# Attention, gated convolution and two-way mixing on one core: new engines and a new order for the channel MLP's preparing work

## The chip, the cores and the metric

The kernel runs on one core of a Trainium2 chip. Five engines work at once, each through its own list of instructions in order: TensorE (PE, matmul; its weight loads are listed as PEld), VectorE (DVE), ScalarE (ACT), GpSimd (POOL) and SyncE (SP, which here only issues transfers). They wait for one another by semaphores. The metric is the device time of one launch in microseconds (us); the median of three runs of the kernel before is 745.95 us. Under 0.2% (1.5 us) two kernels here cannot be told apart.

## The reference

```python
def _attn_ref(q, k, v, s):                    # 4 batches, 8 heads, 576 tokens, 64 wide
    cum = np.cumsum(np.maximum(s, 0.0), axis=-1)
    bias = -(cum[:, :, :, None] - cum[:, :, None, :])
    scores = np.matmul(q, k.transpose(0, 1, 3, 2)) / np.sqrt(D)
    scores = np.where(causal, -1e9, scores + np.minimum(bias, 0.0))
    attn = softmax(scores)
    return np.matmul(attn, v)

def _moe_ref(x, w_val, conv_w, w_out):        # x: 4 x 576 tokens x 512 channels
    gate = sigmoid(causal_conv5(x, conv_w))
    return (gate * (x @ w_val)) @ w_out

def _moe2_ref(x, U, V, w_ch1, w_ch2):         # U 576x32, V 32x576, w_ch1 512x2048
    u = x + (x.transpose(0, 2, 1) @ U @ V).transpose(0, 2, 1)
    return u + np.maximum(u @ w_ch1, 0.0) @ w_ch2
```

Attention's output goes through `_moe_ref`, and that through `_moe2_ref`; everything is float32.

## The kernel before, in words

**Number format.** Each float32 operand of a large product is split into a high and a low part of the type that PE multiplies fast (fp32r). `rnd` (L187) rounds to the high part, `rest` (L198) takes the low part, and a product is three matmuls: high by high, high by low, low by high (`three`). So each operand costs a rounding and a subtraction on some engine before PE can start on it.

**Stages.** Until about 295 us the 32 heads of attention run (scores `sc`, exponentials `P`, transposes `pt`, `av`), and beside them the dense work of batches that are done: convolution and gate, `w_val` and `w_out`, and the token mixing with U and V (`nh`/`nl` are the split transposes, `ast` the split product with U, then 16 matmuls `d<-V4h,ast` and `d<-V4l,ast`, added to the residual `uT` on line L766). For the last batch the dense work ends near 365 us. Then comes the channel MLP, to the end at 743 us.

**The channel MLP.** The hidden width of 2048 is cut into 16 blocks, two to a group, 8 groups (g). The 2304 tokens are cut into five tiles: 0 to 3 of 512 and tile 4 of 256. For each tile and block, `ch1` makes 12 matmuls into a PSUM tile `d`; ACT takes the relu and rounds (`hh`), DVE takes the rest (`hl`); `ch2` makes 12 matmuls into the four accumulators `acc0` to `acc3`, two blocks behind each other in the same accumulators, and after the second block DVE adds each to `uT` (L1076). `acc0` and `acc1` have two PSUM buffers of their own, `acc2` and `acc3` share the six of `d`. `ch2` runs two blocks behind `ch1` (`LAG`). From group 1 on, tiles 2 and 3 are done together by seven products in place of eight (`seven`). Those need sums of the two tiles' tokens (`token_sums`, L935: names `sn`, and `Th`/`Tl` for their parts; two sets, made once) and sums of quarters of each weight group (`weight_sums`, L957: `Sh`/`Sl`, made for each group).

**The transition.** The blocks of tiles 0 to 2 of group 0 (`EARLY` = 3) are mixed into the last batch's dense work, so that PE has something to do while that work waits for other engines; how many goes by the rates `R2` and `R3`. What is left of group 0, and after it the groups 1 to 7, runs in the closing loop. In that loop `token_sums` is emitted, two steps for each step of the MLP, and `split_u` makes the split parts `u` of tile 2, 3 and 4 when the tile comes up.

**Weights.** A weight arrives as 64-bit numbers and is turned into two fp32r parts by `widen` (L421), nine steps for each of 32 pieces: `wd_a` scales the high words (`scr<-raw`), `wd_lim` limits them, four `wd` steps (L429, L430, L433, L434) shift and mask, then `wd_hi` rounds (`w1h` or `w2h`), `wd_rest` takes what is left (`scr<-scr,w1h`) and `wd_lo` adds the low word (`w1l`, `w2l`). 28 of these pieces are made in the MLP, beside PE's work.

**What sets the order.** Each operation has a kind. The table `PLAN` gives every kind an engine and a priority offset, `FIRST` another one during the first heads; the class `Via` (L171) looks it up as the operation is emitted. A scheduler then lays all instructions out by a timeline and these priorities, and each engine executes its list in that order, waiting at the first instruction that is not ready. Helper lines: L185 issues with a priority, L192 and L196 are `rnd` on ACT and on POOL, L201 is `rest`.

Of the kernel before, what the change touches and what calls it, by code (L numbers as in the profile page):

```python
# [21 lines left out]

PLAN = {'pace': ['gpsimd', 6000],
 'qk_hi': ['gpsimd', 100],
 'qk_lo': ['gpsimd', 100],
 'put': ['sync', 3000],
 'wd_rest': ['gpsimd', 0],
 'xh': ['gpsimd', 2000],
 'xl': ['gpsimd', -2000],
 'gh': ['scalar', -2000],  # L30
 'gl': ['vector', 0],
 'uh': ['gpsimd', 0],
 'ul': ['gpsimd', -6000],
 'u4': ['vector', 0],
 'wd_a': ['gpsimd', 0],
 'wd_lim': ['gpsimd', -2000],
 'wd': ['vector', 0],
# [16 lines left out]
 'rb': ['scalar', -100],
 'x': ['vector', -500],
 'tap0': ['scalar', -6000],
 'tap': ['vector', 100],
# [5 lines left out]
 'nh': ['scalar', 0],
 'nl': ['vector', 100],
 'ah': ['scalar', 2000],
 'al': ['vector', 500],
# [69 lines left out]
DT = {'exp': 1.05,
 'xh': 0.32,
 'xl': 0.73,
 'tap': 1.81,
 'taps': 0.44,  # L140
 'tanh': 2.68,
 'gv': 4.87,
 'nl': 1.45,
 'rows': 8.01,
 'prep': 3.36}
# [1066 lines left out]
```

## Time and profile before

| | |
|---|---|
| Runs, us | 745.33, 745.95, 745.99; median 745.95 |
| Profiled execution, us | 745.39, of which the span of the instructions is 743.6 |
| Mean granted clock of PE | 0.993 of full speed |
| Busy share of the span | PE 97%, PEld 82%, DVE 70%, ACT 39%, POOL 53% |

The profile comes from the one execution of 745.39 us. Its span runs from the first to the last instruction; 1.8 us lie around it. A granted clock of 1.00 is 2.4 GHz, one of 0.50 is 1.2 GHz. Busy time of POOL is rough. `out<-in` names what an instruction writes and reads.

### The profile page before, as it was taken

Reading aid. Unit: us, or ns where it says so; the run is one execution under the profiler, and the core shown is the slowest. Engines: PE = TensorE matmul, PEld = TensorE weight load, DVE = VectorE, ACT = ScalarE, POOL = GpSimd, SP = SyncE. Lnnn points to the kernel's source line nnn. Section 1 sums busy time; section 2 is a strip of 40 time slices with the busy share of each in tenths; the row PEclk is TensorE's granted clock in tenths of the full one; section 3 lists DMA queues with packets and bytes.
Section 4 is the critical chain, followed back from the end, with each engine's and each line's share of the span. In section 5 each row is a group of like instructions: output and inputs, shape, how many; then the busy total and the mean of one; then the engine's idle time right before and its main releaser. Section 6 shows DMA issues by size and latency. Waiting matters only on the chain.

```text
span 743.6 us, 12205 instructions
## 1 busy us (share of the span) xinstructions
PE 721.1 (97%) x4327; PEld 609.3 (82%) x4327; DVE 519.4 (70%) x1148; ACT 292.1 (39%) x761; POOL 393.0 (53%) x435
## 2 busy tenths in 40 slices
PE   8898999999999999999979999999999999999998
PEld 5666888789988998898758888888888888888887
DVE  6897988898678656751798696876847657475354
ACT  6677566766687677422221212111212112111120
POOL 2778677666544243640386768757728357181000
PEclk9999999999999999999989999999999999999999
DMA  4665455654556341100001121211101101100023
GB/s 115 200 191 150 121 142 125 161 131 123 138 144 163 91 100 35 58 30 1 1 0 61 53 61 54 85 41 54 49 28 58 57 28 51 37 1 0 15 99 142
DMA packets 27000, 59.38 MB, mean 80 GB/s; under 512 B 4648, under 2 KB 5288, under 8 KB 26940
## 3 DMA queue, kind: packets, MB, share of 16 engines
q1 hardware_dynamic: 26940, 58.61, 27.8%
q8 instruction: 34, 0.56, 0.3%
q14 instruction: 26, 0.21, 0.1%
HBM read 37.04 MB, written 5.31 MB: 57 GB/s over the span
## 4 chain that ended last, share of the span: by engine, by line
PE 82%; DVE 10%; issue 2%; DMA 2%; ACT 2%; POOL 1%; SPq 0%; POOLq 0%; DVEq 0%
PE d L185 38%; PE acc L185 26%; PE pt L185 7%; PE sc L185 5%; PE av L185 5%; DVE av L185 2%; DVE P L185 2%; DVE sn L185 1%; DMA qk<-in_kT 1%; DVE uT L434 1%; DVE Tl L185 1%; ACT P L185 1%; DVE uT L430 0%; DVE uT L1076 0%; DMA uT<-in_w 0%
## 5 line engine op out<-in xcount | busy, mean ns | idle before, releaser
L1076 DVE TENSOR_TENSOR uT<-acc,uT 128x512 f32<-128x512 f32 (+1 forms) x160 | 96.1, 630 | 56.8 <-PE acc L185 56.7
L185 PE MATMUL d<-u,w1h 128*128 128x512 f32 (+1 forms) x464 | 130.2, 366 | 1.1 <-POOL u L185 1.1
L185 PE MATMUL acc<-hl,w2h 128*128 128x512 f32 (+1 forms) x320 | 117.2, 370 | 0.0
L185 PE MATMUL acc<-hh,w2l 128*128 128x512 f32 (+1 forms) x320 | 114.7, 370 | 0.0
L185 PE MATMUL acc<-hh,w2h 128*128 128x512 f32 (+1 forms) x320 | 110.9, 375 | 3.0 <-DVE uT L1076 3.0
L981 ACT ACTIVATE hh<-d 128x512 fp32r<-128x512 f32 (+1 forms) x59 | 31.6, 539 | 186.9 <-PE d L185 147.3
L185 ACT ACTIVATE P<-P,nm 128x576 f32<-128x576 f32 (+4 forms) x160 | 89.1, 559 | 32.7 <-DVE nm L185 32.0
L185 PEld LDWEIGHTS d<-u,w1h 128*128 128x128 f32 x464 | 83.7, 191 | 16.6 <-POOL u L185 2.2
L185 PE MATMUL sc<-K,Q 68*128 68x288 f32 (+13 forms) x384 | 86.6, 338 | 0.3 <-ACT PTA L192 0.2
L185 PE MATMUL d<-u,w1l 128*128 128x512 f32 (+1 forms) x232 | 84.4, 365 | 0.0
L185 PE MATMUL pt<-ident,P 128*128 128x128 f32 x480 | 75.0, 279 | 5.5 <-ACT P L185 3.0
L185 DVE CUSTOM_DVE_ANT_0 P<-sc,causal 64x64 f32<-64x64 f32 (+4 forms) x160 | 64.3, 420 | 22.2 <-PE sc L185 19.1
L185 DVE SCALAR_TENSOR_TENSOR hl<-d,hh 128x512 fp32r<-128x512 f32 (+1 forms) x59 | 36.0, 613 | 58.5 <-ACT hh L981 58.4
L185 PEld LDWEIGHTS acc<-hh,w2h 128*128 128x128 f32 x320 | 60.3, 189 | 14.9 <-issue 3.3
L185 PEld LDWEIGHTS acc<-hh,w2l 128*128 128x128 f32 x320 | 59.8, 188 | 11.6
L185 PEld LDWEIGHTS acc<-hl,w2h 128*128 128x128 f32 x320 | 60.1, 188 | 11.2
L185 PEld LDWEIGHTS sc<-K,Q 68*128 68x128 f32 (+2 forms) x384 | 61.6, 191 | 8.6 <-issue 1.3
L185 PEld LDWEIGHTS pt<-ident,P 128*128 128x128 f32 x480 | 55.2, 142 | 12.2 <-ACT P L185 5.0
L185 DVE SCALAR_TENSOR_TENSOR av<-X,cw,av 128x576 f32<-128x576 f32 x64 | 52.2, 815 | 2.5 <-ACT av L185 2.1
L185 PEld LDWEIGHTS d<-u,w1l 128*128 128x128 f32 x232 | 44.2, 191 | 7.4
L185 POOL TENSOR_SCALAR w2h<-scr 128x512 fp32r<-128x512 f32 x14 | 10.1, 723 | 72.9 <-PE acc L185 53.1
L185 POOL TENSOR_TENSOR Q<-qk,hi 128x576 fp32r<-128x576 f32 x22 | 31.7, 1439 | 16.8 <-PE sc L185 16.8
(170 smaller groups left out, 1587.1 us busy)
## 6 DMA issues: line engine op xcount, KB each, us to landing
raw<-in_w SPq DMA_DIRECT2D x28, 512.0 KB
K<-hi SPq DMA_DIRECT2D x44, 144.0 KB
...
```

The source lines that it names most:

```text
L185: return f(*args, **kw)
L434: lambda: Via("wd").scalar_tensor_tensor(t, raw[..., 0], 2.0 ** -52, t, op0=ALU.mult, op1=ALU.mult),
L981: Via("hh").activation(h_, o, AF.Relu)
L1076: Via("acc").tensor_add(u, o, u)
```

## The change

A third table, `LAST`, holds for what is emitted after the last head, that is for `split_u` and the whole MLP. By it the rounding of the token parts (`uh`), the first step of widening (`wd_a`) and the rounding of weights (`wd_hi`) go from POOL to ACT, and the step behind the rounding (`wd_rest`) from POOL to DVE. In `PLAN` the low part of the weight sums (`sl`) goes from DVE to POOL. Token sums are emitted one step for each MLP step instead of two (`PACE`). Group 0 takes tile 4 before tile 3, and groups 2 to 7 take the tiles in the order 0, 1, 2, 3, 4 instead of 0, 2, 3, 1, 4; group 1 had that order already. Most priorities are new, as are the numbers `R2`, `R3`, `SIDE` and `DT`, by which work is mixed. The kind `tm` of the token mixing's matmuls is split into `tu` (U) and `tv` (V). The arithmetic is the same, and PE and SP have as many instructions as before. ACT gets 72 more and DVE 18 more, POOL 90 fewer. Up to the end of attention PE's order is the same but for a few neighbours that change places. Cut to what the text speaks of:

```diff
-PLAN = {'pace': ['gpsimd', 6000],
+PLAN = {'pace': ['gpsimd', 2000],
...
- 'uh': ['gpsimd', 0],
+ 'uh': ['gpsimd', 6000],
 'ul': ['gpsimd', -6000],
...
- 'wd_lim': ['gpsimd', -2000],
+ 'wd_lim': ['gpsimd', 2000],
 'wd': ['vector', 0],
 'wd_hi': ['gpsimd', -2000],
...
- 'hl': ['vector', -100],
+ 'hl': ['vector', -6000],
 'acc': ['vector', 0],
- 'tc': ['vector', -100],
- 'th': ['scalar', 0],
- 'tl': ['vector', 500],
+ 'tc': ['vector', 500],
+ 'th': ['scalar', -500],
+ 'tl': ['vector', 2000],
...
- 'sl': ['vector', 100],
- 'sn': ['scalar', 2000],
+ 'sl': ['gpsimd', 100],
+ 'sn': ['scalar', 0],
...
-R2 = 0.38
-R3 = 9.68
+R2 = 0.27
+R3 = 10.65
...
-PLACE = [[0, 1, 2, 3, 4], [0, 2, 3, 1, 4]]
+PACE = 1
+PLACE = [[0, 1, 2, 4, 3], [0, 1, 2, 3, 4], [0, 1, 2, 3, 4]]
...
+LAST = {'uh': ['scalar', 500],
+ 'wd_a': ['scalar', -6000],
+ 'wd_hi': ['scalar', 0],
+ 'ox': ['scalar', -2000],
+ 'pt20': ['vector', 500],
+ 'rb': ['vector', 2000],
+ 'c2': ['tensor', -6000],
+ 'acc': ['vector', -100],
+ 'sh': ['scalar', -6000],
+ 'c1': ['tensor', -2000],
+ 'sc': ['gpsimd', -500],
+ 'nh': ['scalar', 100],
+ 'wd_rest': ['vector', 0],
+ 'wd': ['vector', 6000],
+ 'pt30': ['vector', 2000]}
...
-            self.name, self.ahead = FIRST.get(kind, PLAN[kind]) if PLAN[kind][0] != "sync" and phase[0] <= 8 else PLAN[kind]
+            self.name, self.ahead = FIRST.get(kind, PLAN[kind]) if PLAN[kind][0] != "sync" and phase[0] <= 8 else LAST.get(kind, PLAN[kind]) if phase[0] == NH else PLAN[kind]
...
-        for t in range(NB) if g == 0 else PLACE[g > 1]:
+        for t in PLACE[min(g, 2)]:
...
-            for _ in range(2):
+            for _ in range(PACE):
...
-        assert i < 2 * D_ + 1 or not sums2
+        assert i < 2 * PLACE[0].index(D_) + 2 or not sums2
```

The lists below are the engines' orders as built; lines of the changed kernel lie 26 further down.

**PE, ahead of the last batch's V stage** (`d<-V4h,ast`). `acc_4905` and `acc_4921` belong to tile 1, `acc_5045` and `acc_5051` to tile 2. Before:

```order
L185 MATMUL d<-nh,U_68 128x512
L185 MATMUL d<-nl,U_68 128x512
L185 MATMUL acc_5045<-hh,w2h 128x512
L185 MATMUL acc_5045<-hl,w2h 128x512
L185 MATMUL acc_5045<-hh,w2l 128x512
L185 MATMUL d<-nh,U_68 128x512
L185 MATMUL acc_5051<-hh,w2h 128x512
L185 MATMUL acc_5051<-hl,w2h 128x512
L185 MATMUL acc_5051<-hh,w2l 128x512
L185 MATMUL d<-nl,U_68 128x512
L185 MATMUL d<-V4h,ast 128x288
```

After (`acc_4932`, `acc_4936` belong to tile 1):

```order
L211 MATMUL acc_4932<-hh,w2h 128x512
L211 MATMUL acc_4936<-hh,w2h 128x512
L211 MATMUL d<-nh,U_68 128x512
L211 MATMUL acc_4932<-hl,w2h 128x512
L211 MATMUL acc_4936<-hl,w2h 128x512
L211 MATMUL acc_4932<-hh,w2l 128x512
L211 MATMUL acc_4936<-hh,w2l 128x512
L211 MATMUL d<-nl,U_68 128x512
L211 MATMUL d<-V4h,ast 128x288
```

Tile 2's six `acc` matmuls, and 12 of its `ch1` matmuls a little further up, are no longer ahead of the V stage but behind it.

**ACT, from the last batch's `ast` on.** `u` are the high parts of tiles 3 and 4, `Sh` here a buffer that holds a high part of tile 3. Before:

```order
L185 ACTIVATE ast<-d 128x512
L192 ACTIVATE Th_4989<-sn_5005 128x512
L192 ACTIVATE Th_4993<-sn_5007 128x512
L192 ACTIVATE Th_4991<-sn_5006 128x512
L981 ACTIVATE hh<-d 128x512
L192 ACTIVATE Th_4994<-sn_5069 128x512
L192 ACTIVATE Th_4990<-sn_5067 128x512
L192 ACTIVATE Th_4995<-sn_5006 128x512
L981 ACTIVATE hh<-d 128x512
```

After:

```order
L211 ACTIVATE ast<-d 128x512
L211 ACTIVATE u_4419<-uT 128x256
L211 ACTIVATE u_4421<-uT 128x256
L1007 ACTIVATE hh<-d 128x512
L211 ACTIVATE Sh_4985<-uT 128x512
L211 ACTIVATE u_5009<-uT 128x256
L211 ACTIVATE Sh_4985<-uT 128x512
L211 ACTIVATE u_5128<-uT 128x512
L218 ACTIVATE w1h<-scr_5070 128x512
L211 ACTIVATE Th_4989<-sn_5005 128x512
L211 ACTIVATE u_5011<-uT 128x256
L211 ACTIVATE u_5130<-uT 128x512
```

The roundings of `u` and of `w1h` stood in POOL's list before and stand in ACT's now, among the `Th`.

**DVE, up to the first add of an accumulator of tile 2** (`acc_5045` before, `acc_5042` after). Before:

```order
L185 TENSOR_TENSOR sn_5067<-uT,u_4868 128x512
L185 TENSOR_TENSOR Tl_4999<-sn_5006,Th_4991 128x512
L185 SCALAR_TENSOR_TENSOR hl<-d,hh 128x512
L185 TENSOR_TENSOR sn_5069<-uT 128x512
L185 TENSOR_TENSOR sn_5067<-sn_5067,u_4869 128x512
L185 TENSOR_TENSOR sn_5006<-u_4870,sn_5006 128x512
L185 TENSOR_TENSOR Tl_5002<-sn_5069,Th_4994 128x512
L185 TENSOR_TENSOR sn_5006<-sn_5006,u_4871 128x512
L185 TENSOR_TENSOR Tl_4998<-sn_5067,Th_4990 128x512
L1076 TENSOR_TENSOR uT<-acc_5045,uT 128x512
L185 TENSOR_TENSOR Tl_5003<-sn_5006,Th_4995 128x512
```

After:

```order
L211 TENSOR_TENSOR sn_5006<-sn_5006,u_4887 128x512
L211 TENSOR_TENSOR Tl_5002<-sn_5126,Th_4994 128x512
L211 SCALAR_TENSOR_TENSOR hl<-d,hh 128x256
L211 SCALAR_TENSOR_TENSOR scr_5108<-scr_5108,scr_5109 128x512
L211 TENSOR_TENSOR Tl_4998<-sn_5124,Th_4990 128x512
L211 SCALAR_TENSOR_TENSOR hl<-d,hh 128x256
L211 TENSOR_TENSOR Tl_5003<-sn_5006,Th_4995 128x512
L211 TENSOR_SCALAR scr_5109<-scr_5108 128x512
L211 TENSOR_TENSOR sn_5125<-uT,sn_5124 128x512
L211 SCALAR_TENSOR_TENSOR scr_5109<-raw,scr_5109 128x512
L227 TENSOR_TENSOR scr_5108<-scr_5108,w2h 128x512
L211 TENSOR_TENSOR uT<-acc_5042,uT 128x512
L211 SCALAR_TENSOR_TENSOR hl<-d,hh 128x512
```

Before, nothing of `widen` stands ahead of that add; after, the widening of a second weight does (`scr_5108`, `scr_5109`), with `wd_rest` now on DVE.

## Rows read from the trace of the kernel before

**Rows 1.** The page: busy us, share of the span, instructions of each engine.

```profile
PE 721.1 (97%) x4327; PEld 609.3 (82%) x4327; DVE 519.4 (70%) x1148; ACT 292.1 (39%) x761; POOL 393.0 (53%) x435
```

**Rows 2.** Windows: engine busy us (instructions), then granted clock, DMA share, GB/s.

```profile
34.00:37.28 3.28, 2.27 (x10) 1.39 (x10) 3.28 (x10) 2.20 (x8) 3.20 (x4) 1.00 0.60 146
37.28:40.69 3.41, 3.29 (x18) 2.41 (x19) 2.55 (x9) 2.58 (x10) 3.22 (x5) 0.50 0.42 101
295.00:325.00 30.00, 28.60 (x211) 26.03 (x210) 23.15 (x51) 12.91 (x32) 17.78 (x20) 1.00 0.16 50
363.00:387.70 24.70, 20.75 (x95) 16.25 (x95) 24.08 (x30) 4.77 (x8) 22.71 (x21) 0.95 0.00 1
385.44:392.26 6.82, 5.20 (x18) 4.26 (x19) 6.82 (x13) 1.53 (x5) 3.05 (x3) 0.50 0.00 0
400.00:740.00 340.00, 340.00 (x1646) 283.88 (x1645) 221.74 (x352) 59.18 (x104) 172.62 (x168) 1.00 0.15 50
```

**Rows 3.** Waits of PE, whole span: us in total, times, longest us.

```profile
PE acc L185 <- DVE uT L1076: 3.0, 3, 2.4
```

**Rows 4.** Timeline of PE, 361 to 389 us: start us, us, instruction, [idle before <-releaser].

```profile
361.16 0.39 PE L185 MATMUL acc<-hh,w2l 128*128 128x512 f32 x1
361.39 0.40 PE L185 MATMUL d<-nl,U 128*128 128x512 f32 x1
363.20 0.40 PE L185 MATMUL d<-V4h,ast 128*128 128x288 f32 x1 [1.41 <-DVE ast L185]
...
379.83 0.50 PE L185 MATMUL d<-u,w1h 128*128 128x512 f32 x1 [0.31 <-POOL u L185]
...
382.65 0.50 PE L185 MATMUL d<-u,w1h 128*128 128x512 f32 x1 [0.80 <-POOL u L185]
...
386.71 0.76 PE L185 MATMUL acc<-hh,w2h 128*128 128x512 f32 x1 [2.41 <-DVE uT L1076]
387.82 1.65 PE L185 MATMUL acc<-hh,w2h 128*128 128x512 f32 x3 [0.35 <-DVE uT L1076]
```

**Rows 5.** Timeline of DVE, 384 to 387 us.

```profile
384.22 1.75 DVE L185 TENSOR_TENSOR Tl<-sn,Th 128x512 fp32r<-128x512 f32 x1
385.89 0.68 DVE L1076 TENSOR_TENSOR uT<-acc,uT 128x512 f32<-128x512 f32 x1
386.49 0.68 DVE L185 TENSOR_TENSOR Tl<-sn,Th 128x512 fp32r<-128x512 f32 x1
```

**Rows 6.** Windows, only instructions that write or read tile sn (DVE's token sums).

```profile
363.00:387.70 24.70, 18.37 (x15) 3.79 (x6) 0.95 0.00 1
```

**Rows 7.** Windows, only the instructions of line L196.

```profile
363.00:387.70 24.70, 6.76 (x9) 0.95 0.00 1
```

**Rows 8.** Groups on POOL, 363 to 387.7 us: busy us, mean ns, idle before.

```profile
L201 POOL TENSOR_TENSOR scr<-scr,w1h 128x512 f32<-128x512 f32 x1 | 1.3, 1300 | 0.0
...
L185 POOL TENSOR_SCALAR w1h<-scr 128x512 fp32r<-128x512 f32 x1 | 1.1, 1134 | 0.0
```

**Rows 9.** Groups on DVE, 361 to 397 us.

```profile
L434 DVE SCALAR_TENSOR_TENSOR scr<-raw,scr 128x512 f32<-128x512 uint32 x1 | 1.4, 1447 | 0.0
...
L185 DVE SCALAR_TENSOR_TENSOR hl<-d,hh 128x256 fp32r<-128x256 f32 x2 | 0.8, 408 | 0.0
```

**Rows 10.** Groups on POOL, 400 to 720 us.

```profile
L201 POOL TENSOR_TENSOR scr<-scr,w2h 128x512 f32<-128x512 f32 x13 | 20.0, 1541 | 1.4 <-DVE scr L433 0.4
...
L185 POOL TENSOR_SCALAR w2h<-scr 128x512 fp32r<-128x512 f32 x13 | 9.1, 702 | 69.4 <-PE acc L185 53.1 <-DVE scr L430 16.1
```

**Rows 11.** Groups on ACT, 400 to 720 us.

```profile
L185 ACT ACTIVATE Sh<-scr 128x512 fp32r<-128x512 f32 x14 | 8.8, 632 | 18.1 <-POOL scr L185 18.1
```

**Rows 12.** Timeline of ACT, 266 to 324 us.

```profile
268.96 0.78 ACT L185 ACTIVATE P<-P,nm 128x576 f32<-128x576 f32 x1 [1.53 <-DVE nm L185]
...
321.42 0.41 ACT L185 ACTIVATE gvh<-d 128x288 fp32r<-128x288 f32 x1 [0.82 <-DVE d L185]
```

More of the change, by code (lines that the diff above doesn't have):

```diff
@@ L20 @@
 DRAM = bass.MemoryType.DRAM
-PLAN = {'pace': ['gpsimd', 6000],
- 'qk_hi': ['gpsimd', 100],
+PLAN = {'pace': ['gpsimd', 2000],
+ 'qk_hi': ['gpsimd', 0],
  'qk_lo': ['gpsimd', 100],
- 'put': ['sync', 3000],
+ 'put': ['sync', 100],
  'wd_rest': ['gpsimd', 0],
- 'xh': ['gpsimd', 2000],
- 'xl': ['gpsimd', -2000],
- 'gh': ['scalar', -2000],
+ 'xh': ['gpsimd', 500],
+ 'xl': ['gpsimd', -500],
+ 'gh': ['scalar', -100],
  'gl': ['vector', 0],
- 'uh': ['gpsimd', 0],
+ 'uh': ['gpsimd', 6000],
  'ul': ['gpsimd', -6000],
@@ L42 @@
  'exp': ['scalar', -2000],
- 't': ['tensor', 500],
- 'pt00': ['scalar', 0],
+ 't': ['tensor', 0],
+ 'pt00': ['scalar', -6000],
  'pt10': ['scalar', 6000],
- 'pt20': ['scalar', 500],
+ 'pt20': ['scalar', -2000],
  'pt30': ['scalar', 2000],
@@ L50 @@
  'av': ['tensor', 6000],
- 'rs': ['vector', 500],
- 'wrs': ['gpsimd', 6000],
+ 'rs': ['vector', -500],
+ 'wrs': ['gpsimd', 100],
  't_rb': ['tensor', 2000],
[L54 to L57, printed above, removed]
+ 'rb': ['scalar', 500],
+ 'x': ['vector', 2000],
+ 'tap0': ['scalar', 0],
+ 'tap': ['vector', -6000],
  'tanh': ['scalar', -2000],
  'd': ['tensor', -6000],
- 'gv': ['vector', 2000],
- 'ox': ['scalar', -2000],
+ 'gv': ['vector', -2000],
+ 'ox': ['scalar', 0],
  'tm': ['tensor', 500],
[L63 to L66, printed above, removed]
+ 'nh': ['scalar', 100],
+ 'nl': ['vector', -500],
+ 'ah': ['scalar', 500],
+ 'al': ['vector', -2000],
  'um': ['vector', 0],
  'c1': ['tensor', 100],
- 'c2': ['tensor', -500],
+ 'c2': ['tensor', -6000],
  'hh': ['scalar', 0],
- 'hl': ['vector', -100],
+ 'hl': ['vector', -6000],
  'acc': ['vector', 0],
- 'tc': ['vector', -100],
- 'th': ['scalar', 0],
- 'tl': ['vector', 500],
+ 'tc': ['vector', 500],
+ 'th': ['scalar', -500],
+ 'tl': ['vector', 2000],
  'sc': ['gpsimd', 2000],
- 'sh': ['scalar', 2000],
- 'sl': ['vector', 100],
- 'sn': ['scalar', 2000],
- 'sa': ['vector', 6000]}
+ 'sh': ['scalar', -100],
+ 'sl': ['gpsimd', 100],
+ 'sn': ['scalar', 0],
+ 'sa': ['vector', 6000],
+ 'tu': ['tensor', 500],
+ 'tv': ['tensor', 2000]}
 R0 = 0.34
 R1 = 0.0
-R2 = 0.38
-R3 = 9.68
+R2 = 0.27
+R3 = 10.65
 DENSE = 36.0
@@ L95 @@
 XB = 1
-FIRST = {'pt41': ['scalar', -6000],
+FIRST = {'pt41': ['scalar', 2000],
  'nl': ['vector', 500],
@@ L101 @@
  'rs': ['vector', 500],
- 't': ['tensor', -2000],
+ 't': ['tensor', -100],
  'rb': ['vector', -6000],
  'av': ['tensor', 6000],
- 'wd_rest': ['gpsimd', 2000],
+ 'wd_rest': ['gpsimd', -100],
  'ah': ['scalar', 0],
@@ L109 @@
  'xl': ['gpsimd', 500],
- 'pt40': ['scalar', -2000],
- 'gv': ['vector', 0],
+ 'pt40': ['scalar', -6000],
+ 'gv': ['vector', -6000],
  'd': ['tensor', 100],
- 'pt00': ['scalar', 0],
+ 'pt00': ['scalar', -2000],
  'gl': ['vector', -2000],
@@ L117 @@
  'wd_hi': ['gpsimd', -6000],
- 'u4': ['vector', -500],
- 'pt20': ['scalar', -6000],
+ 'u4': ['gpsimd', -500],
+ 'pt20': ['scalar', 2000],
  'pace': ['gpsimd', 500],
  'tm': ['tensor', -6000],
- 'tap': ['vector', -2000],
+ 'tap': ['vector', 2000],
  'qk_lo': ['gpsimd', -100],
@@ L125 @@
  'um': ['vector', 2000],
- 'wd_lim': ['gpsimd', -6000],
+ 'wd_lim': ['gpsimd', 6000],
  'c1': ['tensor', 2000],
  'sa': ['vector', 100],
- 'pt30': ['scalar', 0],
- 'tc': ['vector', -100],
+ 'pt30': ['scalar', -6000],
+ 'tc': ['gpsimd', -100],
  'sn': ['scalar', 500],
- 'sh': ['scalar', -500]}
+ 'sh': ['vector', -500],
+ 'tu': ['tensor', -6000],
+ 'tv': ['tensor', -6000],
+ 'qk_hi': ['gpsimd', 100],
+ 'th': ['scalar', 500],
+ 'wd_a': ['gpsimd', -100],
+ 'nh': ['scalar', -500],
+ 'ox': ['scalar', -100],
+ 'wd': ['vector', 0]}
 ORDER0 = 'T0 S0 T1 T4 S1 T3 T2 S2 S3 S4'
 ORDER = 'T0 S0 T1 T2 T3 S1 S2 S3 T4 S4 A0 A1'
-NPD = 6
[L136 to L143, printed above, removed]
+LAST = {'uh': ['scalar', 500],
[4 more added lines that the diff above has]
+ 'rb': ['vector', 2000],
+ 'c2': ['tensor', -6000],
+ 'acc': ['vector', -100],
+ 'sh': ['scalar', -6000],
+ 'c1': ['tensor', -2000],
+ 'sc': ['gpsimd', -500],
+ 'nh': ['scalar', 100],
+ 'wd_rest': ['vector', 0],
+ 'wd': ['vector', 6000],
+ 'pt30': ['vector', 2000]}
+NPD = 6
+DT = {'exp': 1.99,
+ 'xh': 0.11,
+ 'xl': 0.91,
+ 'tap': 1.98,
+ 'taps': 0.77,
+ 'tanh': 1.61,
+ 'gv': 4.0,
+ 'nl': 2.33,
  'rows': 8.01,
- 'prep': 3.36}
+ 'prep': 4.3}
 WARM = 13
@@ L751, in outputs @@
             lhsT = U4[:, c, :, :].rearrange("p a r -> p (a r)")
-            Via("tm").matmul(acc, lhsT, nh, start=(c == 0), stop=False)
-            Via("tm").matmul(acc, lhsT, nl, start=False, stop=(c == 4))
+            Via("tu").matmul(acc, lhsT, nh, start=(c == 0), stop=False)
+            Via("tu").matmul(acc, lhsT, nl, start=False, stop=(c == 4))
             yield 0.44
@@ L762, in outputs @@
                 lhsT = a[:, m * P:(m + 1) * P]
-                Via("tm").matmul(ps[:, 0:HS], lhsT, V4["h"][:, cols], start=True, stop=False)
-                Via("tm").matmul(ps[:, 0:HS], lhsT, V4["l"][:, cols], start=False, stop=True)
+                Via("tv").matmul(ps[:, 0:HS], lhsT, V4["h"][:, cols], start=True, stop=False)
+                Via("tv").matmul(ps[:, 0:HS], lhsT, V4["l"][:, cols], start=False, stop=True)
                 u = uT[:, m, b * S + hf * HS:b * S + hf * HS + HS]
```

2 lines of the change are left out of this document (1 added, 1 removed).

## The prediction

> **What bounds the kernel now.** I read the page first: PE is busy 97% of the span, every other engine 70% or less [rows 1]. So only what leaves PE idle, or slows its clock, can move the time. The windows tell where that is. From 400 to 740 us PE is busy 340.00 of 340 us at full clock, with DVE at 222, POOL at 173 and ACT at 59 [rows 2]: nothing is to be gained there, and something to lose only if another engine becomes late. From 295 to 325 us PE lacks 1.4 us, and from 363 to 387.7 us 4 us; behind that, from 385.44 to 392.26 us, it runs at half clock [rows 2]. The waits name the cause: PE waited 3.0 us for L1076, DVE's adds of the accumulators, 2.4 of it at once [rows 3]. The timeline gives the order: after the V stage begins (363.20) PE waits 0.31 and 0.80 for POOL's `u`, then 2.41 and 0.35 for DVE [rows 4]. DVE's timeline shows why that add was late: it ended at 386.49, right behind a `Tl` that took 1.75 us, where the next one took 0.68 [rows 5]. DVE was busy 24.08 of 24.7 us there and POOL 22.71 [rows 2]. So one stretch, 363 to 392 us, holds almost all that this change can give.
>
> **What that stretch costs.** Matmuls with 512 columns start 0.23 us apart (361.16, 361.39) [rows 4]; I take 0.232, and by columns 0.133 for 288 and about 0.118 for 256. From the first V matmul to the first `acc` matmul that has to wait for DVE the old order has 66, 16 and 12 of these: 15.3 + 2.1 + 1.4 = 18.9 us. It took 386.71 - 363.20 = 23.5 [rows 4], so 4.65 us were lost, and 0.35 at the next wait: 5.0. The half clock costs half of PE's busy 5.20 us in its window [rows 2]: 2.6. Together 7.6 us.
>
> **The V stage comes earlier.** 18 matmuls of 512 columns move from ahead of the V stage to behind it: 18 x 0.232 = 4.2 us. In itself that is no gain, since PE's sum is the same, but the token sums, which need the V stage, start 4.2 us sooner relative to PE's other work, which now covers them. The wait for `ast` (1.41) [rows 4] is left as it is: the same chain of ACT and DVE, two adds of tile 1 now ahead of DVE's part (at most 0.25 us more), against one short wait of 0.27 for an accumulator just before, which goes with tile 2's matmuls.
>
> **Until DVE is needed.** With tile 4 ahead of tile 3, the first `acc` matmul that waits for an add (`acc0` of tile 4) has 84, 16 and 35 matmuls before it: 19.5 + 2.1 + 4.1 = 25.7 us after the V stage began, against 18.9. DVE must have added `acc_5042` by then. Before, the add ended 386.49 - 363.20 = 23.3 us after that point. The new list puts ahead of it one `sn`, one `Tl` and one `hl` more (0.68 each, the undisturbed `Tl` [rows 5]: 2.0), two `hl` of 256 columns (0.41 each [rows 9]: 0.8), the four `wd` steps of a weight (one is 1.45 [rows 9], the others about 1.5 together: 2.9) and two `wd_rest`. On DVE `wd_rest` isn't in the trace; it subtracts like `sn` and `Tl`, so it costs between 0.68 and 1.75 [rows 5]; I take 1.1 each, as POOL will be busy less: 2.2. That is 8.0 us, less 0.08 for each of the 11, as neighbours overlap (384.22 + 1.75 against 385.89 [rows 5]): 7.1.
>
> **What POOL gives back.** The 15 `sn` and `Tl` up to 387.7 us took 18.37 us [rows 6]; undisturbed they are 15 x 0.68 = 10.2. So 8.2 us were lost beside POOL's work. Of POOL's 22.71 us [rows 2] the change takes away line L196's 6.76 (six `u`, two `Sh`, one `scr<-raw`) [rows 7], one `w1h` and one `wd_rest` (2.4) [rows 8]: 9.2, or 40%. By that share 3.3 us come back; the ends are 0 (POOL's subtractions alone still block DVE) and 8.2. The add then ends at 23.3 + 7.1 - 3.3 = 27.1, PE goes on 0.2 later (386.49 to 386.71) at 27.3: 1.6 us lost instead of 4.65. I add 0.2 for the adds behind it and keep 1.8. POOL's waits are in the 4.65: the high parts on ACT cost 0.6 each [rows 11], ACT was busy 4.77 of 24.7 us [rows 2], and POOL has only the low parts left, which PE needs later than before for tile 3. ACT's cover there is its idle time; if it were gone, each late `hh` would cost PE 0.6.
>
> **The clock.** It fell after the one long gap, 2.41 us. With the gap cut to about 1.6 I expect it not to fall: 2.6 us gained; the ends are 0 and 2.6.
>
> **ACT in attention.** Some 14 roundings of `u` come between 255 and 325 us onto ACT, which executes in order: the exponentials and `gvh` behind them wait with them. From 295 to 325 us ACT is busy 12.91 of 30 us [rows 2], and it idles 1.53 before one exponential and 0.82 before a `gvh` [rows 12], so most of the 14 x 0.6 us falls into gaps. One, near 266 us, has to wait for a transfer that reads the buffer it will write, and holds back the exponentials by about 1.6 us; PE takes those some 6 us later. Ends: 0.5 us gained (POOL freer) to 1.5 lost; I take 0.3 lost. SP's list differs by two loads that change places with neighbours; what waits for them has long been ahead: 0.
>
> **The steady part.** Over 400 to 720 us POOL loses 26 `wd_rest` (1.54 each) [rows 10], which cost DVE 26 x 0.68 to 1.5, or 18 to 39 us, less about 10 for `Sl`. DVE's 222 of 340 us become at most 251. ACT takes some 49 roundings at 0.63 [rows 11]: 31 us, 59 to 90. PE covers both, at 340 of 340. The cover is thinnest at `w2h`: on POOL it waited 53.1 us in all for PE to release the old weight [rows 10], and on ACT `hh` is queued behind it. The list has each `w2h` behind the `hh` that PE needs to get to that release, so I cost it at 0. The tile order of groups 2 to 7 is that of group 1, which runs without a wait in the windows: 0.
>
> **Sum.** 745.39 (the profiled execution: span 743.6 and 1.8 around it) - (5.0 - 1.8) - 2.6 + 0.3 = 739.9 us. It stands 0.56 under the median of the runs, so the forecast is **740.4 us**.
>
> **Rivals.** *B: the clock falls all the same*, 740.4 + 2.6 = 743.0 us (742.0 to 744.4). For it: near 37 us it fell after two waits under 1 us, with PE busy 2.27 of 3.28 us [rows 2], so one long gap isn't needed. Against it: with PE at 28.60 of 30 us (295 to 325) it held, and the 1.41 of 363.20 did nothing [rows 2, 4]. The Trainium skill (TensorE: Matmul & The Clock Gate, section "A second HAM failure mode: psum-queue depth-cycling") says that many tiny idles between groups of matmuls can toggle the clock too; the stretch before 37.28 agrees, the one at 295 us doesn't, and by that rule the time is B's.
> *C: nothing comes of it*, 744.5 to 747.4 us, about 745.9: the cover gained is eaten by DVE's new work, as with nothing back from POOL (27.1 + 3.3 + 0.2 = 30.6 against 25.7: 4.9 lost) and the clock falling as before.
> *D: slower. DVE becomes the bound of the transition.* If POOL gives back nothing and each `wd_rest` pays 1.75, the add ends at 31.7 and PE loses 6.2 and more, against 5.0; with a gap that long the half clock lasts longer by up to as much again (0 to 2.6), and ACT's 0.3 comes on top. 745.95 + 1.5 + 1.3 + 0.3 = 749.0 us (747.5 to 752). It decides from about 30.8 us on for that add. For it: DVE has no idle time there [rows 2], and gets more work. Against it: 40% of POOL's work goes. A rule speaks for it: by the Trainium skill (SBUF — State Buffer, section "Who interferes with whom") a DVE instruction with two SBUF inputs contends with a POOL instruction that reads SBUF, as `wd_rest` now will, while ACT never waits for anyone's port. The trace agrees in kind (1.75 against 0.68, and 0.68 for the add, which reads PSUM [rows 5]).
> *E: the order is not what the engines meet*, so that POOL's low parts or ACT are late in another place: within C's times.
>
> **Chances.** Forecast A (738.0 to 742.0) 0.52, B 0.17, C and E 0.14, D 0.17. A difference of 0.2%, 1.5 us, is about what a measurement of this kernel can tell from none: faster means under 744.5, slower over 747.4. Faster 0.69, same 0.14, slower 0.17. The low end takes all waits and the clock as gone and attention's 0.5 as gained: 745.95 - 5.0 - 2.6 - 0.5 = 737.8. The range runs from there through A, B and C to D's start, 737.8 to 747.5; D, and a rest of 0.03 below, lie outside.
>
> **What the changed profile would show.** Right: between the V stage and 392 us no wait of PE over 1.7 us, waits for `u` gone, `Tl` nearer 0.68 than 1.2, granted clock 1.00 behind it, POOL busy some 60% there, windows from 400 us on still full. Wrong: a wait for L1076 as long as before or a window at 0.50 after it (B, C, D); new waits `pt<-ACT P` between 260 and 290 us; PE below 20 of 20 in a window of groups 1 to 7, waiting for `hh` or for `w1h`.

## The result, and the profile after

The changed kernel takes **739.5 us** (median of 6 runs, 738.73 to 740.53) against 745.97 us before (6 runs): a ratio of 0.9914, with a 95% interval of 0.9901 to 0.9927. The forecast was 740.4 us. The profiled execution took 739.28 us, its span is 737.5.

The page's first part, busy us, share and instructions (before: [rows 1]):

```profile
PE 716.9 (97%) x4327; PEld 605.8 (82%) x4327; DVE 522.0 (71%) x1166; ACT 331.8 (45%) x833; POOL 307.8 (42%) x345
```

POOL lost 85 us of work, ACT got 40, DVE 3. Windows of the changed kernel, with the columns of [rows 2]; the third is the stretch from the V stage to 0.6 us behind the first `acc` matmul of tile 4 that needs DVE's add:

```profile
34.00:41.00 7.00, 5.14 (x31) 3.34 (x31) 6.82 (x21) 5.54 (x17) 6.73 (x8) 1.00 0.58 148
295.00:325.00 30.00, 28.74 (x214) 26.39 (x213) 26.43 (x58) 16.26 (x37) 15.43 (x14) 1.00 0.10 37
359.53:386.50 26.97, 26.84 (x140) 22.79 (x141) 26.07 (x39) 11.67 (x23) 14.61 (x11) 1.00 0.04 11
386.50:400.00 13.50, 13.50 (x64) 10.95 (x64) 13.36 (x24) 3.54 (x6) 3.71 (x4) 1.00 0.17 58
400.00:734.00 334.00, 334.00 (x1609) 278.28 (x1608) 215.87 (x353) 86.94 (x152) 105.74 (x104) 1.00 0.15 50
```

PE is busy 26.84 of 26.97 us where it lacked 4 us before, and its clock holds behind that. POOL is busy 54% there, DVE still nearly all of the time. From 400 us on PE stays full, with ACT at 87 and POOL at 106 us. All waits of PE from 355 to 735 us (columns as in [rows 3]):

```profile
PE d L211 <- DVE ast L211: 1.6, 1, 1.6
PE acc L211 <- ACT hh L1007: 0.2, 1, 0.2
```

The waits for L1076's adds and for `u` [rows 3, 4] are gone. How close it was is seen on PE's and DVE's timelines. PE, with the V stage's first matmul and, at 385.88, the first one that needs the add of `acc_5042`:

```profile
359.53 0.40 PE L211 MATMUL d<-V4h,ast 128*128 128x288 f32 x1 [1.64 <-DVE ast L211]
...
385.76 0.28 PE L211 MATMUL acc<-hh,w2l 128*128 128x256 f32 x1
385.88 0.28 PE L211 MATMUL acc<-hh,w2h 128*128 128x256 f32 x1
```

DVE, with the two `wd_rest` (L227) and that add (384.99):

```profile
368.66 1.19 DVE L227 TENSOR_TENSOR scr<-scr,w1h 128x512 f32<-128x512 f32 x1
...
384.39 0.68 DVE L227 TENSOR_TENSOR scr<-scr,w2h 128x512 f32<-128x512 f32 x1
384.99 0.68 DVE L211 TENSOR_TENSOR uT<-acc,uT 128x512 f32<-128x512 f32 x1
385.59 0.68 DVE L211 SCALAR_TENSOR_TENSOR hl<-d,hh 128x512 fp32r<-128x512 f32 x1
```

The add ended 385.59 - 359.53 = 26.1 us after the V stage began, and PE came to it at 26.35: 0.3 us to spare, or 0.1 if PE needs the 0.2 us that it took before from the add to the matmul (386.49 to 386.71, [rows 4, 5]). The `sn` and `Tl` of that stretch (columns as in [rows 6]):

```profile
359.53:386.50 26.97, 15.90 (x17) 4.29 (x7) 1.00 0.04 11
```

That is 0.94 us each, against 18.37 / 15 = 1.22 before [rows 6]. ACT's timeline shows the roundings it took over, one behind the other while POOL and DVE were both busy, none slowed:

```profile
364.44 0.62 ACT L211 ACTIVATE Sh<-uT 128x512 fp32r<-128x512 f32 x1
364.96 0.41 ACT L211 ACTIVATE u<-uT 128x256 fp32r<-128x256 f32 x1
365.27 0.62 ACT L211 ACTIVATE Sh<-uT 128x512 fp32r<-128x512 f32 x1
```

**Where the 6.1 us of span went.** The V stage began at 359.53 instead of 363.20: 3.7 us earlier, where 4.2 us of work had been moved behind it, so 0.5 us were lost up to there. One matmul in attention tells where; it is the same one in PE's order (before, then changed):

```profile
248.24 0.30 PE L185 MATMUL d<-xl,wvh 128*128 128x288 f32 x1
248.54 0.30 PE L211 MATMUL d<-xl,wvh 128*128 128x288 f32 x1
```

So 0.3 us were lost ahead of it, less than executions differ by there (see T below), and behind it 0.2: 359.53 - 248.54 + 4.2 = 115.2 us to the V stage against 363.20 - 248.24 = 115.0.

From the V stage to the end it took 737.5 - 359.53 = 378.0 us against 743.6 - 363.2 = 380.4, with those 4.2 us more in it: 6.6 us gained.

### The profile page after: what moved, and what is told of

It is laid out like the page before. It is cut to its first block, busy times and chain, and to the rows that moved or that the text cites. A ratio compares the mean times of both kernels' runs of the same rounds, so it can differ in the third digit from the quotient of the medians.

```text
span 737.5 us, 12144 instructions
## 1 busy us (share of the span) xinstructions
PE 716.9 (97%) x4327; PEld 605.8 (82%) x4327; DVE 522.0 (71%) x1166; ACT 331.8 (45%) x833; POOL 307.8 (42%) x345
## 4 chain that ended last, share of the span: by engine, by line
PE 83%; DVE 9%; DMA 3%; ACT 2%; issue 2%; POOL 1%; SPq 1%; POOLq 0%; DVEq 0%
PE d L211 39%; PE acc L211 26%; PE sc L211 6%; PE av L211 5%; PE pt L611 4%; PE pt L211 3%; DVE P L211 1%; DVE av L211 1%; DVE sn L211 1%; DVE Tl L211 1%; DVE uT L460 1%; DMA uT<-in_w 1%; ACT P L211 1%; DMA qk<-in_kT 1%; SPq L211 0%
## 5 line engine op out<-in xcount | busy, mean ns | idle before, releaser
L211 DVE TENSOR_TENSOR uT<-acc,uT 128x512 f32<-128x512 f32 (+1 forms) x160 | 94.6, 629 | 50.1 <-PE acc L211 50.0
L211 PE MATMUL acc<-hl,w2h 128*128 128x512 f32 (+1 forms) x320 | 107.5, 370 | 0.0
L211 PE MATMUL acc<-hh,w2h 128*128 128x512 f32 (+1 forms) x320 | 105.1, 371 | 0.2 <-ACT hh L1007 0.2
L211 PE MATMUL acc<-hh,w2l 128*128 128x512 f32 (+1 forms) x320 | 104.5, 371 | 0.0
L211 POOL TENSOR_TENSOR w2l<-scr,scr 128x512 fp32r<-128x512 f32 x14 | 18.1, 1296 | 110.7 <-DVE scr L227 83.4
L611 PE MATMUL pt<-ident,P 128*128 128x128 f32 x360 | 55.0, 276 | 2.8 <-DVE nm L211 1.4
L611 PEld LDWEIGHTS pt<-ident,P 128*128 128x128 f32 x360 | 41.0, 141 | 6.4 <-issue 1.5
L211 POOL TENSOR_TENSOR u<-uT,u 128x512 fp32r<-128x512 f32 (+1 forms) x18 | 23.5, 1324 | 53.4 <-ACT u L211 42.6
```

The lines of the kernel that those rows point to most:

```text
L211: return f(*args, **kw)
L611: Via("t").transpose(ps[:, (j - b0) * P:(j - b0 + 1) * P], Pt[c][n % PB[c]][:, j * P:(j + 1) * P], ident)
```

## Experiments

For comparing kernels I use that second number besides the time: **T**, the time from the first matmul of the last V stage to the end of the span, less 4.2 us where the 18 matmuls of tile 2 lie behind the V stage. T of before is 380.4, of the changed kernel 373.8. It leaves out attention, in which one execution differs from another: the matmul that runs at 248.54 us in the changed kernel ran at 247.37 in experiment 3 and at 248.70 in experiment 11, though the lists of the three are the same up to there and the clock of all three was 1.00 from 6 us to it. From that matmul on executions agree much better: the changed kernel and experiments 2, 8, 9 and 11 took 110.95 to 110.99 us from it to the V stage. T comes from one profile of each kernel, and that execution is the fastest of its kernel in experiments 3, 9 and 10; where the slower ones of those lost their time no profile tells. Four of them (the changed kernel, 4, 10 and 11) have the same transition but for priorities, and their T lies between 373.6 and 373.8.

| | kernel | median, us | ratio to before, 95% | V stage, span | T |
|---|---|---|---|---|---|
| | before | 745.97 | | 363.20, 743.6 | 380.4 |
| | changed | 739.5 | 0.9914 (0.9901 to 0.9927) | 359.53, 737.5 | 373.8 |
| 1 | changed, old rates | 741.04 | 0.9947 (0.9926 to 0.9967) | 363.13, 739.3 | 376.2 |
| 2 | changed, tile 3 ahead of 4 | 741.84 | 0.9945 (0.9924 to 0.9965) | 360.55, 739.6 | 374.9 |
| 3 | changed, old engines | 750.2 | 1.0062 (1.0041 to 1.0083) | 358.05, 746.3 | 384.1 |
| 4 | changed, old attention tables | 740.38 | 0.9942 (0.9924 to 0.9960) | 359.95, 737.8 | 373.7 |
| 5 | before, new engines | 744.22 | 0.9989 (0.9974 to 1.0004) | 364.76, 742.6 | 377.8 |
| 6 | before, new rates | 746.51 | 1.0021 (1.0007 to 1.0035) | 358.92, 743.9 | 380.8 |
| 7 | changed, `u` and `Sh` on POOL | 746.76 | 1.0016 (1.0006 to 1.0026) | 358.53, 745.0 | 382.3 |
| 8 | changed, widening on POOL | 746.12 | 1.0015 (0.9999 to 1.0030) | 359.21, 743.2 | 379.8 |
| 9 | changed, `wd_rest` on POOL | 741.47 | 0.9929 (0.9901 to 0.9957) | 358.80, 737.7 | 374.7 |
| 10 | before, engines + rates + tile 4 | 742.59 | 0.9948 (0.9927 to 0.9969) | 360.74, 738.5 | 373.6 |
| 11 | changed, old tile order from group 2 | 739.34 | 0.9908 (0.9883 to 0.9933) | 359.68, 737.6 | 373.7 |
| 12 | changed, gap at `ast` filled | 742.88 | 0.9952 (0.9937 to 0.9967) | 361.59, 739.9 | 378.3 |

The medians of 1 to 4, 5 to 8 and 9 to 12 were taken at three times, each beside runs of the kernel before, so the ratios are what compares.

**Two theories.** Theory 1, cover: the gain comes from PE work moved behind the V stage, which hides DVE's token sums. Theory 2, engines: it comes from POOL's work that went away, so that POOL and DVE no longer block one another. The prediction's sum has both as terms.

**1, the rates back.**

```diff
-R2 = 0.27
-R3 = 10.65
+R2 = 0.38
+R3 = 9.68
```

> The changed kernel with only the two mixing rates R2 and R3 put back, so that 18 matmuls of tile 2 (4.2 us) stand ahead of the last batch's V stage again; engines and tile order stay changed. Theory 1 (cover): in the changed kernel DVE's add of the first accumulator ended 26.1 us after the V stage began and PE needed it at about 25.9, so there is no slack; with 4.2 us less work behind the V stage PE waits about 4 us for that add. 743.5 us if the clock holds, up to 746 if the gap lets it fall. Theory 2 (engines): what counts is that POOL no longer slows DVE; the time stays within 1.5 us of 739.5.

T grew by 2.4 us, with two waits of about 1.0 us for `hl`, one at 381 us and one at 430. The time, 741.0, lies below what theory 1 expected and at the edge of theory 2; by the ratios it is 2.5 us above the changed kernel, as T says. So cover is worth something, but 2.4, not 4, since the scheduler also moved DVE's list: the add ended at 384.68 - 363.13 = 21.5 us after the V stage began, 4.5 earlier than in the changed kernel, with the last two `wd` steps of the second weight and its `wd_rest` now behind it.

```profile
384.07 0.68 DVE L211 TENSOR_TENSOR uT<-acc,uT 128x512 f32<-128x512 f32 x1
```

**2, tile 3 ahead of tile 4 again.**

```diff
-PACE = 1
-PLACE = [[0, 1, 2, 4, 3], [0, 1, 2, 3, 4], [0, 1, 2, 3, 4]]
+PACE = 2
+PLACE = [[0, 1, 2, 3, 4], [0, 1, 2, 3, 4], [0, 1, 2, 3, 4]]
```

> The changed kernel with group 0 in the old tile order 0, 1, 2, 3, 4 (the step count PACE set to 2, which by the built lists alters nothing by itself). Theory 1 (cover): PE meets the first accumulator that needs DVE's add some 2.8 to 7 us of work earlier, so it waits 2.5 to 5 us: 742 to 744.5 us, up to 747 if the clock falls too. Theory 2 (engines): within 1.5 us of 739.5.

T grew by 1.1 us, less than theory 1's 2.5; the time lies between the two theories. `PACE` itself does nothing: with 2 in the place of 1 the changed kernel's built lists are the same on all engines, so it got no run of its own.

**3, the engines back.**

```diff
- 'sl': ['gpsimd', 100],
+ 'sl': ['vector', 100],
...
-LAST = {'uh': ['scalar', 500],
- 'wd_a': ['scalar', -6000],
- 'wd_hi': ['scalar', 0],
+LAST = {'uh': ['gpsimd', 0],
...
- 'wd_rest': ['vector', 0],
```

> The changed kernel with uh, wd_a, wd_hi and wd_rest back on POOL and sl back on DVE; rates, tile order and the other priorities stay changed. Theory 1 (cover, with POOL's contention as a term): sn and Tl go from 0.94 to about 1.2 us each, 17 of them, so 4.9 us later, less two wd_rest of about 0.9 that leave DVE: the add ends 3 us later, 742.5 us, 745 if the clock falls. Theory 2 (engines): all of the gain goes, 745 to 747 us. A third, that cover alone does it: within 1.5 us of 739.5.

It is slower than before, and by more than any theory said: T 384.1, 10.3 us above the changed kernel. Waits of PE from 355 to 420 us, then its timeline and DVE's around the add, then the windows behind it:

```profile
PE acc L208 <- DVE uT L208: 5.9, 3, 4.6
PE d L208 <- DVE ast L208: 1.6, 1, 1.6
```

```profile
358.05 0.40 PE L208 MATMUL d<-V4h,ast 128*128 128x288 f32 x1 [1.64 <-DVE ast L208]
...
385.13 0.77 PE L208 MATMUL acc<-hh,w2h 128*128 128x256 f32 x2 [4.61 <-DVE uT L208]
```

```profile
378.50 3.45 DVE L208 TENSOR_TENSOR Tl<-sn,Th 128x512 fp32r<-128x512 f32 x2
...
384.30 0.68 DVE L208 TENSOR_TENSOR uT<-acc,uT 128x512 f32<-128x512 f32 x1
```

```profile
384.00:405.00 21.00, 18.56 (x79) 14.90 (x80) 17.64 (x32) 2.52 (x5) 10.29 (x10) 0.84 0.15 51
```

The add ended at 384.90, 26.9 us after the V stage, only 0.8 later than in the changed kernel; but PE had come to it after 385.13 - 4.61 - 358.05 = 22.5 us, as the list was laid out in another way. That wait and the next two are 5.9 us; the clock of 0.84 over 21 us is 6.7 us at half speed, about 3 us more. So this cover, with the old engines, is no gain at all.

**4, attention's tables back.**

```diff
-SIDE = [10, 8, 4, 6]
+SIDE = [8, 8, 3, 6]
```

`PLAN`, `FIRST` and `DT` take the values of before in the same way, and `LAST` is filled up with the changed values of `PLAN`, so that they hold from `split_u` on.

> The changed kernel with the tables PLAN, FIRST, DT and SIDE of before for all that is emitted up to the last head; from split_u on the changed tables hold. In the changed kernel the V stage began only 3.7 us earlier, where 4.2 us of work had been moved behind it and 1.7 us of an early half clock near 37 us were missing, so attention itself became about 2.1 us longer. If that is the new priorities' doing: 737.4 us when the clock near 37 us holds, 739 when it falls there as it did before. If it is scatter: 739.5, within 0.7.

T is the same and the time neither lower nor clearly higher; runs of this kernel lay between 739.17 and 745.91 us. So the V stage's lost 0.5 us are not the new priorities' doing. They even save about 1.0 us late in attention: the matmul of 248.54 us ran at 247.99 here, and from it to the V stage it took 359.95 - 247.99 = 111.96 us, against 110.95 to 110.99 with the new ones.

**5, the engines alone.**

```diff
+LAST = {'uh': ['scalar', 500],
+ 'wd_a': ['scalar', -6000],
+ 'wd_hi': ['scalar', 0],
+ 'wd_rest': ['vector', 0],
+ 'sl': ['gpsimd', 100]}
...
-            self.name, self.ahead = FIRST.get(kind, PLAN[kind]) if PLAN[kind][0] != "sync" and phase[0] <= 8 else PLAN[kind]
+            self.name, self.ahead = FIRST.get(kind, PLAN[kind]) if PLAN[kind][0] != "sync" and phase[0] <= 8 else LAST.get(kind, PLAN[kind]) if phase[0] == NH else PLAN[kind]
```

> The kernel before with only the engines moved after the last head (uh, wd_a, wd_hi to ACT, wd_rest to DVE, sl to POOL); rates, tile order, priorities as before. Theory 2 (engines decide): it keeps most of the gain. From the V stage to the end the kernel before spent 10.0 us more than PE's own work, the changed one 3.4; with old rates but new engines and tile order it was 5.8, so here about 7: 742.3 us (741 to 743.5). Theory 1 (cover decides): 744 to 746, as DVE now also has wd_rest without more PE work to hide it.

T fell by 2.6 us, about the 3 that theory 2 expected, with `hl` now the wait (1.6 us) instead of the add. The time didn't follow: its interval holds no change, and 744.2 lies where theory 1 had it. A part was lost ahead of the V stage, which began 1.6 us later than before. From the matmul of 248.24 us (here 247.05) to it took 117.7 us, 2.7 more than before; some 1.7 of that are a stretch at half clock near 301 us, and the other 1.0 is what experiment 4 also lost with the old priorities.

**6, the rates alone.**

```diff
-R2 = 0.38
-R3 = 9.68
+R2 = 0.27
+R3 = 10.65
```

> The kernel before with only the rates R2 and R3 changed, so that the V stage comes 4.2 us earlier. Theory 1 (cover decides): the waits shrink by up to 4 us and the half clock goes: 740 to 742 us. Theory 2 (engines decide): POOL and DVE block one another all through the transition, so that the add comes as late as before or later counted from the V stage: 744.5 to 748 us, as with the engines put back in the changed kernel (13.7 us over PE's work from the V stage on).

Theory 1 falls as far as cover alone goes. PE's timeline has one wait, longer than before, and the clock falls behind it:

```profile
358.92 0.40 PE L185 MATMUL d<-V4h,ast 128*128 128x288 f32 x1 [1.42 <-DVE ast L185]
...
387.56 1.94 PE L185 MATMUL acc<-hh,w2h 128*128 128x512 f32 x3 [5.26 <-DVE uT L1076]
```

```profile
359.00:385.00 26.00, 23.30 (x112) 19.16 (x112) 24.73 (x29) 5.96 (x11) 22.59 (x21) 1.00 0.00 1
385.00:400.00 15.00, 12.30 (x50) 9.45 (x51) 12.35 (x23) 2.41 (x6) 7.51 (x8) 0.78 0.18 60
```

PE came to the add after 387.56 - 5.26 - 358.92 = 23.4 us, 2.3 later than before (386.71 - 2.41 - 363.20 = 21.1, with its short waits for `u`), but the add came 5.1 later, at 28.4 us: the list has four more `sn` and `Tl`, one more `hl` and two `wd` steps ahead of it, and POOL, busy 22.59 of 26 us, held DVE up as before.

That holding up goes by the engines and not by the cover. This is the time of the `sn` and `Tl` from the V stage to the add, with the old engines (before, 6, 3) and with the new ones (changed, 5); columns as in [rows 6]:

```profile
363.20:385.89 22.69, 17.62 (x14) 3.79 (x6) 0.99 0.00 1
358.92:386.74 27.82, 20.59 (x18) 4.42 (x7) 0.97 0.00 1
358.05:384.30 26.25, 19.78 (x17) 4.42 (x7) 1.00 0.00 1
359.53:384.99 25.46, 15.59 (x16) 4.29 (x7) 1.00 0.00 1
364.76:387.52 22.76, 14.01 (x15) 3.75 (x6) 1.00 0.00 1
```

One takes 1.26, 1.14 and 1.16 us with the old engines, 0.97 and 0.93 with the new.

**7 and 8, half of the engines back.** First `uh` alone:

```diff
-LAST = {'uh': ['scalar', 500],
+LAST = {'uh': ['gpsimd', 0],
```

> The changed kernel with only uh (the high parts u and Sh) back on POOL. By POOL's time in the stretch, 5.2 of the 9.2 us that were moved come back, so over half of the 10.7 us that all engine moves were worth: about 745 us (743.5 to 747), with a wait for L1076's add of 2 to 3 us and a window at half clock. Rival (widening decides): within 1.5 us of 739.5.

Then the widening alone:

```diff
- 'wd_a': ['scalar', -6000],
- 'wd_hi': ['scalar', 0],
...
- 'wd_rest': ['vector', 0],
```

> The changed kernel with only the widening (wd_a, wd_hi, wd_rest) back on POOL; u stays on ACT, sl on POOL. By POOL's time 4.0 of 9.2 us come back, but DVE is rid of two wd_rest (1.9 us in the changed profile): 741 to 743 us. Rival (widening decides, since POOL now has sl too and the weights come late in every group): 745 us or more, with PE waiting for w1h or w1l after 400 us.

T rose by 8.5 and by 6.0 us, together more than the 10.3 of experiment 3, which puts back both and `sl`: the moves aren't additive, each is needed. The first came at the time expected, but not by one wait for the add: PE waited for `hl`, `hh` and the add in turn. The clock fell as expected, to a mean of 0.89 from 385 to 400 us.

```profile
379.42 0.50 PE L211 MATMUL acc<-hl,w2h 128*128 128x512 f32 x1 [2.38 <-DVE hl L211]
...
385.65 0.50 PE L211 MATMUL acc<-hh,w2h 128*128 128x256 f32 x2 [2.47 <-ACT hh L1007]
...
387.73 0.39 PE L211 MATMUL acc<-hh,w2h 128*128 128x256 f32 x1 [1.57 <-DVE uT L211]
```

The second was expected at 741 to 743 and missed; its rival fell too, since every window from 400 us on stayed full. PE's timeline of the kernel with the widening on POOL shows several short waits in the transition, and the window behind them:

```profile
378.92 0.50 PE L208 MATMUL acc<-hl,w2h 128*128 128x512 f32 x1 [0.94 <-DVE hl L208]
...
383.80 0.38 PE L208 MATMUL acc<-hh,w2h 128*128 128x256 f32 x1 [1.36 <-ACT hh L1004]
384.81 0.38 PE L208 MATMUL acc<-hh,w2h 128*128 128x256 f32 x1 [0.63 <-DVE uT L208]
386.22 0.51 PE L208 MATMUL acc<-hl,w2h 128*128 128x256 f32 x2 [1.02 <-DVE hl L208]
```

```profile
385.00:400.00 15.00, 13.98 (x64) 11.73 (x64) 13.16 (x24) 1.83 (x3) 8.71 (x9) 0.89 0.21 70
```

**9, `wd_rest` alone back on POOL**, the line `'wd_rest': ['vector', 0],` taken out of `LAST`.

> The changed kernel with wd_rest alone back on POOL. On DVE the two in the transition took 1.19 and 0.68 us; on POOL each takes 1.3 to 1.7, and DVE's two-input instructions meet it there. If only the sum of DVE's own work counts, DVE is 1.9 us earlier and the time stays at 739.5 or 0.5 below; if what POOL holds counts for more than what DVE does itself, 740.5 to 743; if wd_rest was what made the widening on POOL cost 6.6 us (the kernel with all of it back), 744 or more.

T is 0.9 us higher, and the median lies where the second case had it; by the ratios no difference to the changed kernel can be told. So where `wd_rest` runs matters little, and what made experiment 8 slow are the other two steps of the widening, or the three together.

**10, the three parts on the old priorities:** experiments 5 and 6 together, and tile 4 ahead of tile 3 in group 0.

> The kernel before with the three parts together: engines moved after the last head, R2 and R3, tile 4 ahead of tile 3 in group 0; every priority, SIDE and DT and the tile order of groups 2 to 7 as before. If the three parts are the change, 739.5 (738.5 to 740.5), about 3.4 us over PE's work from the V stage on; if the new priorities are needed to make them fit, 742 or more.

T is 373.6, like the changed kernel's: in the profiled execution the three parts do in the transition all that the change does. The time, 742.59, lies higher than the 739.5 expected and where the other case had it (742 or more), by the ratios 2.5 us above the changed kernel. About 1.2 of that is ahead of the V stage: from the matmul of 248.54 us (here 248.57) to it took 112.2 us, against 110.95 to 110.99, as in experiments 4 and 5 with the old priorities. The rest isn't explained: the profiled execution, 740.25, is the fastest of nine, and the five slowest had a mean clock of 0.991 to 0.995, the four fastest 0.998 to 1.000; where they lost it no profile shows. So the new priorities are worth something, in attention at least.

**11, the old tile order from group 2 on,** `[0, 2, 3, 1, 4]` as the last list of `PLACE`.

> The changed kernel with groups 2 to 7 in the old tile order 0, 2, 3, 1, 4. PE is full there in both kernels: 739.5, within 0.7, all windows from 480 us on full. Rival: the new order hides widening that the old one would not with roundings on ACT: waits of PE for w1h or hh after 440 us, 741 or more.

The same time and T: that part of the change does nothing.

**12, an attempt at a better one.**

```diff
-R3 = 10.65
+R3 = 11.8
...
+ 'tl1': ['gpsimd', 2000],
...
-            return [lambda: rnd("th", hi, x), lambda: rest("tl", lo, x, hi)]
+            return [lambda: rnd("th", hi, x), lambda: rest("tl" if k == 0 else "tl1", lo, x, hi)]
```

> An attempt at a better one: the changed kernel with R3 = 11.8, which puts 12 ch1 matmuls of tile 2 back ahead of the V stage and its six acc matmuls between the last U product and the V stage, where PE waited 1.64 us for ast; and the Tl of the second set of token sums on POOL, which was idle for 8.6 us there, so that DVE's first add stands some five instructions earlier in its list. V stage at about 362 us, 4.2 us less work behind it. If DVE's list is what bounds the transition: no wait for ast, under 1 us for the adds, 738.0 (737 to 739). If POOL's Tl block DVE again: waits of 2 to 3 us as with the rates alone put back, 740 to 741.

The wait for `ast` went, and more came in its place. PE's timeline, then DVE's and POOL's at the first of the new waits:

```profile
361.59 0.29 PE L212 MATMUL d<-V4h,ast 128*128 128x288 f32 x1
...
380.88 0.39 PE L212 MATMUL acc<-hl,w2h 128*128 128x256 f32 x1 [1.45 <-DVE hl L212]
```

```profile
379.00 1.49 DVE L212 TENSOR_SCALAR scr<-scr 128x512 uint32<-128x512 uint32 x1
380.41 0.41 DVE L212 SCALAR_TENSOR_TENSOR hl<-d,hh 128x256 fp32r<-128x256 f32 x1
```

```profile
378.62 3.00 POOL L212 TENSOR_TENSOR Tl<-sn,Th 128x512 fp32r<-128x512 f32 x2 [1.29 <-ACT Th L212]
```

A `wd` step that takes 0.41 alone took 1.49 beside POOL's two `Tl`, and the `hl` behind it, for which PE waits, came late. The time, 742.9, lies above both cases expected, though the clock held (1.00 from 385 to 400 us). T is 378.3, and 376.2 in experiment 1, which has the same 18 matmuls ahead of the V stage and its `Tl` on DVE; so in this stretch `Tl` on POOL gained nothing.

## Why the prediction was right

**The sum.** Forecast: 3.2 us of waits, 2.6 of clock, 0.3 lost in attention, 5.5 in all. Measured in the profiles: 6.6 us from the V stage on and 0.5 lost ahead of it, 6.1; by the medians 6.5. The mechanism is the one forecast. The 5.8 from the V stage on (3.2 and 2.6) came 0.8 low, out of two misses that partly cancel; that the total is as close as it is, is in part luck:

- *What that stretch costs* was put at 5.0 of waits, counted from the pace of the matmuls. The waits that the profile names behind the V stage are 4.1: 3.0 for the adds and 1.1 for `u` [rows 3, 4]. In the changed kernel the profile names none there, and 4.1 and the 2.6 of the clock are 6.7, which agrees with the 6.6 measured.
- *Until DVE is needed*: PE's need at 25.7 us was measured at 26.35, and DVE's add, forecast for 27.1, ended at 26.1. So the 1.8 us of waits that the sum kept didn't come. As much as that 1.0 us comes from the widening, which was put too high: the four `wd` steps took 2.2 us instead of 2.9, since the one that had taken 1.45 beside POOL took 0.68, and the two `wd_rest` 1.9 instead of 2.2 (1.19 and 0.68).

```profile
378.84 0.42 DVE L211 TENSOR_SCALAR scr<-scr 128x512 uint32<-128x512 uint32 x1
...
380.71 0.68 DVE L211 SCALAR_TENSOR_TENSOR scr<-scr,scr 128x512 uint32<-128x512 uint32 x1
...
382.85 0.42 DVE L211 TENSOR_SCALAR scr<-scr 128x512 uint32<-128x512 uint32 x1
...
383.79 0.68 DVE L211 SCALAR_TENSOR_TENSOR scr<-raw,scr 128x512 f32<-128x512 uint32 x1
```

- *What POOL gives back*, 3.3 us, was about right: ahead of the add the `sn` and `Tl` took 17.62 us before and 15.59 after (experiment 6), and 17.62, with two more at 0.6 and less 3.3, are 15.5. By the mean of the whole stretch, 1.22 and 0.94 us, it is 0.28 x 15 = 4.2.
- *`wd_rest` on DVE* in the steady part: from 400 us on DVE is busy 216 of 334 us, well below the bound of 251 of 340.
- *The clock* held, as forecast: 1.00 in the windows behind the transition. It isn't the one profile alone: the changed kernel's six runs had a mean clock of 0.997 to 1.000, and the 68 runs of the kernel before that were taken beside the experiments 0.989 to 0.998.
- *ACT in attention*, 0.3 lost: behind the matmul of 248 us, where executions agree, 0.2 was measured. With the old priorities (experiments 4, 5 and 10) it would have been 1.0 to 1.2 more, so it is the new ones, already in the list that the prediction was worked out on, that keep this term small. PE had no wait for `hh` behind the V stage, so the place of `w2h` in ACT's list did no harm. The wait for `ast` grew to 1.64 us, 0.23 more, within the 0.25 allowed.
- *The steady part* and the tile order at 0: PE 334.00 of 334, and experiment 11.
- One of the signs didn't come: `Tl` was to be nearer 0.68 than 1.2 us. Of the six ahead of the add three took 0.68 each, but the other three 4.02 together, which is 1.03 on average.

```profile
370.37 4.02 DVE L211 TENSOR_TENSOR Tl<-sn,Th 128x512 fp32r<-128x512 f32 x3
```

**The rivals.** B (the clock falls all the same) didn't come, but experiment 8 shows its mechanism: a clock of 0.89 behind waits none of which was over 1.36 us. D (slower, with DVE as the bound) is what experiment 3 comes to and, less plainly, 6 to 8; the changed kernel passes it by 0.3 us. Against D the prediction set the share of POOL's work that goes; with that work back the kernel is slower than before (experiment 3), so this was the right place to look. But experiment 3 gets there another way than D's working: its add was not late (26.9 us, where D began at 30.8), PE came to it 3.2 us earlier than the prediction counts for the changed order (22.5 against 25.7). The Trainium skill's rule that spoke for D (SBUF — State Buffer, section "Who interferes with whom": a DVE instruction with two SBUF inputs contends with POOL's reads, ACT with no one) agrees with the traces in kind: 1.19 us for a `wd_rest` beside POOL, 0.68 for one without, and ACT's 0.62 unchanged. But moving `wd_rest` back gains nothing (experiment 9).

**What the sum couldn't tell.** It would give each part its own share, and the parts have none: alone, the rates are worth 0.4 us lost and the engines 2.6 gained in T (experiments 6 and 5); together with tile 4 it is 6.6 to 6.8 (the changed kernel and experiment 10). The working held because it was made on the list as built, with all parts in it.
